# Block-causal attention into two MoE layers on one core: score units regrouped from four a pair to three, one head's evacuation fixed on VectorE, two raw weight tiles given buffers of their own

## The chip, the cores and the metric

The kernel runs on one core of a Trainium2 chip. The metric is the device time of one execution in microseconds (us); three executions of the kernel before are shown below. A core has five engines that run side by side, each in its own program order: TensorE (PE, with its weight loads shown apart as PEld), VectorE (DVE), ScalarE (ACT), GpSimd (POOL) and SyncE (SP), which here issues all the DMAs one after the other.

## The reference

Attention over 576 positions in nine blocks of 64 (a query sees its own block and those ahead of it), then two feed-forward layers with different gates. The outputs of attention are the tokens of the first layer.

```python
q, k, v: (4, 8, 576, 64)                      # batch, heads, positions, head size
scores = q @ k.T / 8
scores = where(pos_q // 64 >= pos_k // 64, scores, -1e9)
attn = exp(scores - max) / (sum + 1e-9)
x = (attn @ v) -> (2304, 512)                 # all heads side by side
h = x @ w_in;  x = (h * clip(h + 3, 0, 6) / 6) @ w_out       # first layer, d_ff 2048
h = x @ w_in2; x = (h * tanh(log1p(exp(h)))) @ w_out2        # second layer, d_ff 2048
```

## The kernel before, in words

All float32 values that go into a product are split in a high and a low part (float32r each); a product is the sum of three: high by high, high by low, low by high.

**Pairs.** The 32 heads of the four batches are taken as 16 pairs: two heads of 64 lie on 128 partitions. For each pair, `load` brings q and k, POOL scales q (L403) and splits q and k into `qs` and `ks` (L406, L290; the first pair's run partly on ACT), `scores` makes the scores of one unit in PSUM (`s`, two buffers), DVE takes the maxima (L443, `nm`), ACT the exponentials with their sums (L448, into `p`), PE transposes the result (L505, into `t`), ACT copies the high part to `z` (L284), DVE subtracts for the low part (L290), PE multiplies by the values (`attn_v`, L569, into the one buffer `o`), and ACT (L582) or DVE (L580) moves `o` to `x`. `sums` handles the sums of the exponentials (L599, L600). `x1d` and `rsd` are the DRAM homes of `x` and of the reciprocals.

**Units.** A pair has four score units. B (queries 128 to 255, keys 0 to 255), AC (queries 256 to 383 with 384 keys, and the first 128 queries with 128 keys) and D (queries 384 to 511, 512 keys) work on half rows: each head's q and k lie on 64 partitions, so a product uses 64 rows of PE's array and two heads run on the two halves. In such a unit the limit of the diagonal blocks is added at its end by a small bfloat16 product (`mask`, L478). E is the last 64 queries: those of the two heads are laid out as a block diagonal `qb` (two small DMAs a pair, 64 partitions x 2 x 64), so that its six products (L455) use all 128 rows.

**Order.** `Schedule` takes the operations in program order and decides by a planner's estimates when each engine issues what; PE's own order may shift by up to 40 operations until the first layer's first output (`plan.strict`). Units are written in the order of `UNITS`; transposes follow 2 units behind, sums 5, products with the values 6 (`LAG_T`, `LAG_R`, `LAG_V`). SP issues the DMAs in one order (L277), and one that waits for its data holds those behind it.

**Weights.** The first layer has 16 weight tiles (f = 0 to 15) that are stored packed, in two halves (c) of 512 KB, and rebuilt by ACT, POOL and DVE. For f = 0 and 1 this happens beside attention in four of the pairs (`early_weights`, `EARLY_ROUNDS`). The tiles f = 2, 3 and 4 (`first_weights`, WLOW is 2 and WMID is 4) go through one pair of raw buffers, `raw0` and `raw1`, one after another; from f = 5 on each has a raw tile that becomes free with attention's memory.

Of the kernel before, what the change touches and what calls it, by code (L numbers as in the profile page):

```python
# [41 lines left out]
E_AT = 224  # L42
ZC = 320

ORDER = tuple(range(NB))
# [5 lines left out]
EARLY_ROUNDS = (20, 28, 36, 44)  # L51
LAG_T, LAG_V, LAG_R = 2, 6, 5
# [14 lines left out]
def cost(kind, n):  # L67

    base, each = {
        "PE": (13, 0.4167), "R": (13, 0.4167), "S": (0, 0.4583), "T": (109, 0), "V": (0, 0.4583),  # L70
        "ACT": (95, 0.836), "ACT_PSUM": (50, 0.836), "EXP": (234, 0.836),
        "DVE_PSUM": (64, 1.047), "DVE": (64, 1.047), "MEMSET": (40, 0.88),
        "POOL": (145, 2.156), "POOL_ONE": (100, 0.99), "POOL_V": (260, 0.87), "SP": (100, 3.05),
    }[kind]
    return max(int(base + each * n), {"S": 105, "V": 105, "R": 215}.get(kind, 0))
# [30 lines left out]
class Schedule:  # L106

    AHEAD = 40

    def __init__(self):
        self.ops, self.writer, self.readers, self.strict = [], {}, {}, 0

# [18 lines left out]
    def order(self):  # L132
# [27 lines left out]
        done = 0  # L160
        port = {"DVE": 0, "POOL": 0}
# [10 lines left out]
        while done < n:  # L172
            best = None
            for e in names:
# [8 lines left out]
                i = min((i for i in c if ready[i] <= start), key=lambda i: (need[i], i))  # L183
                cost = took(i, e, start)
                soon = [k for k in c if start < ready[k] < start + cost and need[k] < need[i]
# [14 lines left out]
            if e == "PE":  # L200
                at += 1
                pe.remove(i)
            done += 1
# [23 lines left out]
def fused_kernel(ctx: ExitStack, tc: tile.TileContext, qT, kT, vv, w1, w2, outT):  # L227
# [75 lines left out]
    sm = pool(late, "sm", 4, side="right")  # L303
# [3 lines left out]
    for n in range(2):  # L307
# [3 lines left out]
        at["qb", n] = aq.tile([P, 2, P], F32R, tag="qb", name=f"qb{n}")  # L311
# [6 lines left out]
        for h in range(2):  # L318
            at["x", h, n] = a2.tile([P, S], F32, tag=f"x{h}", name=f"x{h}_{n}")
# [6 lines left out]
    for n in range(4):  # L326
        for c in range(2):
            at["nm", n, c] = sm.tile([P, 2], F32, tag=f"nm{c}", name=f"nm{c}_{n}")
    for u, w in (("B", 256), ("AC", 512), ("D", 512)):
        at["p", u] = ap.tile([P, 2, w], F32, tag=f"p{u}", name=f"p{u}")  # L330
# [4 lines left out]
    P_NAMES = [("p", u, i, h) for u in GROUPS for i, _, _ in GROUPS[u] for h in range(2)] + [("p", "E"), ("p", "last")]  # L335
# [4 lines left out]
        + [("qb", n, j) for n in range(2) for j in range(2)] + [("mask",), ("ones",), ("hold",)]  # L340
# [6 lines left out]
        + [("nm", n, c) for n in range(4) for c in range(2)]  # L347
# [4 lines left out]

    def load(p):
        n = p % 2
        for j in HALVES if p == 0 else (slice(0, S),):
            js = [i for i in range(2) if j.start <= HALVES[i].start < j.stop]
            for t, src in (("k", kT), ("q", qT)):
                dma((j.stop - j.start) // 2, [], [(t, n, i) for i in js], at[t, n][:, j], src[p, :, j],
                    land=LAND if p else 2600)

    def load_v(p):
        dma(320, [], [("v", p % 2)], at["v", p % 2], vv[p], land=LAND)
# [67 lines left out]
    def scores(g):  # L430
        p, u = g // NU, UNITS[g % NU]
        n, sc = p % 2, at["s", g % 2]
        qs, ks, qb, su = at["qs", n], at["ks", n], at["qb", n], at["su", n]
        half = lambda t, js: [(t, n, i, j) for i in range(2) for j in js]
        nm = [at["nm", g % 4, c] for c in range(2)]

        def maxima(c, view, to):
            width = 1
            for x in view.shape[1:]:
                width *= x  # L440
            plan.add(
                one("DVE", "DVE_PSUM", width), [("s", g % 2)], [("nm", g % 4, c)],
                lambda e: nc.vector.tensor_reduce(to, view, axis=AX.X, op=ALU.max, negate=True))  # L443

        def exps(c, h, w, a, dst, name, col):
            plan.add(
                one("ACT", "EXP", w), [("s", g % 2), ("nm", g % 4, c)], [name, ("su", n, col)],
# [3 lines left out]
        if u == "E":  # L451
            def run(e):
                for a, z in ((E_AT, 512), (512, E_AT + S)):
                    for k, (x, y) in enumerate(((0, 0), (0, 1), (1, 0))):
                        nc.tensor.matmul(  # L455
                            sc[:, a:z], qb[:, x, :], ks[:, y, a - E_AT:z - E_AT], start=k == 0, stop=k == 2)

            matmuls(6 * cost("S", S // 2), [("qb", n, j) for j in range(2)] + half("ks", (0, 1)),
                    [("s", g % 2)], run)
            maxima(0, sc[:, E_AT:E_AT + S], nm[0][:, 0:1])  # L460
            exps(0, 0, S, E_AT, at["p", u][:, 0:S], ("p", u), 8)
# [4 lines left out]
        def run(e):  # L466
            for k, (x, y) in enumerate(((0, 0), (0, 1), (1, 0))):
                for i, a, w in groups:
                    for h in range(2):
                        r = slice(64 * h, 64 * h + 64)  # L470
                        nc.tensor.matmul(
                            wide[:, h, a:a + w], qs[r, x, 128 * i:128 * i + 128], ks[r, y, 0:w],
                            start=k == 0 and a == 0, stop=False, skip_group_check=True)
            for h in range(2):
# [5 lines left out]
                    start=False, stop=True, skip_group_check=True)  # L480

        ns = sum(3 * cost("R", w) for _, _, w in groups) + 250
        js = (0,) if u == "B" else (0, 1)
        matmuls(ns, half("qs", js) + half("ks", js) + [("mask",), ("ones",)], [("s", g % 2)], run)
        for c, (i, a, w) in enumerate(groups):
            maxima(c, wide[:, :, a:a + w], nm[c])
        for c, (i, a, w) in enumerate(groups):
            for h in range(2):
                exps(c, h, w, 512 * h + a, at["p", u][:, h, a:a + w], ("p", u, i, h), 4 * h + i)
# [24 lines left out]
    def transposes(g):  # L514
        p, u = g // NU, UNITS[g % NU]
        n = p % 2
        z, x = at["z", n], at["p", u]
        chunk = lambda a: a.rearrange("p (c w) -> p c w", w=ZC)
        four = lambda tp: tp[:, 0:4, :]
        if u == "E":  # L520
# [3 lines left out]
            transpose_unit(  # L524
                n, u, 0, [x[:, c * P:c * P + P] for c in range(4)], [("p", u)], lambda tp: heads(tp, 4),
                [d[:, 0:4] for d in dst])
            plan.add(
                one("POOL", "POOL_ONE", 64), [("p", u)], [("p", "last")],
# [3 lines left out]
                n, u, 1, [x[:, 512:S + 64]], [("p", u), ("p", "last")], lambda tp: heads(tp, 1), [dst[0][:, 4:5]] * 2, slice(64, P))  # L532
        elif u == "B":
            blocks = [x[:, h, c * P:c * P + P] for h in range(2) for c in range(2)]
            transpose_unit(
                n, u, 0, blocks, [("p", u, 1, h) for h in range(2)],
                lambda tp: tp.rearrange("p (h c) q -> p h (c q)", h=2),
                [z[:, t, :, 4 * ZC:4 * ZC + 256] for t in range(2)])
        else:
            at_ = 0 if u == "AC" else P  # L540
            for h in range(2):
                transpose_unit(
                    n, u, h, [x[:, h, c * P:c * P + P] for c in range(4)],
                    [("p", u, i, h) for i, _, _ in GROUPS[u]], four,
                    [chunk(z[:, t, h])[:, 0:4, at_:at_ + P] for t in range(2)])

    def attn_v(p, r, h):
# [27 lines left out]
        a, w = ((0, 256), (256, 320))[r]  # L575
        dst, src = x[:, a:a + w], po[:, 0:w]
# [7 lines left out]
        plan.add(one("ACT", "ACT_PSUM", w) + one("DVE", "DVE_PSUM", w), [("o",)], [("x", h, n, r)], evacuate)  # L584
# [677 lines left out]
```

## Time and profile before

| what | value |
|---|---|
| median of three executions | 942.04 us (941.57 to 942.71) |
| profiled execution, its own time | 944.14 us |
| its span in the trace | 942.4 us |
| granted clock over it | 0.999 |
| PE busy | 917.9 us, 97% of the span |
| DVE busy | 606.8 us, 64% |
| POOL busy | 606.8 us, 64% |
| ACT busy | 531.9 us, 56% |

The time of an execution is a little longer than the span from the trace's first to its last instruction (944.14 against 942.4). Busy shares are means over stages with different limits: attention is the first sixth of the span, and the two layers are the rest.

### The profile page before, as it was taken

The page shows a single profiled execution, that of the slowest core. Times are in us where ns is not written, and L with a number is a line of the kernel's source. Part 1 is how long each engine was busy: PE and PEld are TensorE (multiplying, and loading weights), DVE is VectorE, ACT ScalarE, POOL GpSimd, SP SyncE. Part 2 cuts the span into 40 slices and gives each one's busy share as a digit, 9 for nine tenths or more (in the row PEclk, how much of TensorE's full clock was granted, in tenths as well). Part 3 has the DMA queues.
Part 4 walks back from the last instruction along what each step waited for, and adds up shares of the span by engine and source line. Part 5 has one row for each costly group of instructions (what it writes and reads, how often), then busy time and mean ns, then how long its engine had stood idle before and what let it go on. Part 6 is the DMA issues. An engine that isn't in the chain of part 4 may idle for free.

```text
span 942.4 us, 16053 instructions
## 1 busy us (share of the span) xinstructions
PE 917.9 (97%) x5368; PEld 830.9 (88%) x5368; DVE 606.8 (64%) x1043; ACT 531.9 (56%) x1232; POOL 606.8 (64%) x625
## 2 busy tenths in 40 slices
PE   8999999989999999999999999999999999999998
PEld 6888888868888777888888899999999999999998
DVE  6788877667954666576422244665687856866567
ACT  7899999856743546455322252644465445644452
POOL 6886775758996548645500022668798787966775
PEclk9999999999999999999999999999999999999999
DMA  6676663498287889988500038767678876696752
GB/s 209 190 224 177 165 178 87 126 312 342 102 246 263 307 272 303 314 290 281 181 1 1 0 100 295 243 247 268 228 286 315 288 268 241 250 319 241 267 207 96
DMA packets 93746, 205.61 MB, mean 218 GB/s; under 512 B 14944, under 2 KB 32992, under 8 KB 93664
## 3 DMA queue, kind: packets, MB, share of 16 engines
q1 hardware_dynamic: 93664, 204.59, 64.7%
q8 instruction: 42, 0.69, 0.3%
q14 instruction: 40, 0.33, 0.1%
HBM read 155.19 MB, written 48.31 MB: 216 GB/s over the span
## 4 chain that ended last, share of the span: by engine, by line
PE 49%; DVE 2%; POOL 2%; DMA 2%; issue 1%; ACT 1%; SPq 0%; DVEq 0%; POOLq 0%; ACTq 0%
PE y L732 8%; PE y L733 8%; PE y L734 8%; PE h L732 5%; PE h L733 5%; PE h L734 5%; PE r L732 3%; PE r L734 3%; PE r L733 3%; DMA w2d<-q 1%; POOL S L290 1%; DVE r L633 0%; DVE S L904 0%; DMA xs<-x1d 0%; POOL q L290 0%
## 5 line engine op out<-in xcount | busy, mean ns | idle before, releaser
L732 PE MATMUL h<-X,wh 128*128 128x512 f32 (+1 forms) x320 | 119.3, 373 | 2.8 <-DVE gl L290 1.2
L734 PE MATMUL h<-X,wl 128*128 128x512 f32 (+1 forms) x320 | 117.9, 368 | 1.0 <-DVE wl L785 1.0
L732 PE MATMUL y<-gh,wh 128*128 128x512 f32 (+1 forms) x320 | 117.9, 369 | 0.9 <-ACT gh L284 0.7
L733 PE MATMUL y<-gl,wh 128*128 128x512 f32 (+1 forms) x320 | 117.8, 368 | 1.0 <-POOL gl L290 1.0
L733 PE MATMUL h<-X,wh 128*128 128x512 f32 (+1 forms) x320 | 117.8, 368 | 0.0
L734 PE MATMUL y<-gh,wl 128*128 128x512 f32 (+1 forms) x320 | 117.7, 368 | 0.0
L732 PE MATMUL y<-X,wh 128*128 128x384 f32 x336 | 112.5, 335 | 1.1 <-ACT xs L284 0.9
L733 PE MATMUL y<-X,wh 128*128 128x384 f32 x336 | 112.5, 335 | 0.0
L734 PE MATMUL y<-X,wl 128*128 128x384 f32 x336 | 112.3, 334 | 0.0
L290 POOL TENSOR_TENSOR X<-xr,X 128x384 fp32r<-128x384 f32 (+2 forms) x36 | 39.3, 1095 | 104.7 <-ACT X L284 104.5
L838 DVE SCALAR_TENSOR_TENSOR h<-e,h 128x512 f32<-128x512 f32 (+1 forms) x64 | 40.1, 627 | 86.3 <-ACT e L284 86.2
L1072 DVE TENSOR_TENSOR sgh<-y,sgh 128x384 f32<-128x384 f32 x129 | 69.6, 555 | 32.9 <-PE y L734 32.8
L284 ACT ACTIVATE e<-h 128x512 f32<-128x512 f32 (+1 forms) x80 | 44.0, 550 | 69.3 <-PE h L734 69.3
L290 POOL TENSOR_TENSOR X<-e,X 128x384 fp32r<-128x384 f32 x69 | 70.9, 1028 | 10.9 <-ACT X L284 10.9
L290 DVE TENSOR_TENSOR z<-t,z 128x512 fp32r<-128x512 f32 (+1 forms) x112 | 67.8, 631 | 14.8 <-ACT z L284 13.5
L443 DVE TENSOR_REDUCE nm<-s 128x2 f32<-128x512 f32 (+4 forms) x80 | 63.1, 797 | 18.9 <-PE s L455 13.1
L732 PEld LDWEIGHTS h<-X,wh 128*128 128x128 f32 x320 | 60.3, 188 | 16.2 <-DVE gl L290 4.0
L732 PEld LDWEIGHTS y<-gh,wh 128*128 128x128 f32 x320 | 60.3, 189 | 11.7 <-ACT gh L284 1.1
L734 PEld LDWEIGHTS h<-X,wl 128*128 128x128 f32 x320 | 60.3, 188 | 11.5 <-DVE wl L785 1.4
L733 PEld LDWEIGHTS y<-gl,wh 128*128 128x128 f32 x320 | 60.3, 188 | 11.1 <-POOL gl L290 1.3
L734 PEld LDWEIGHTS y<-gh,wl 128*128 128x128 f32 x320 | 60.3, 189 | 10.0
L733 PEld LDWEIGHTS h<-X,wh 128*128 128x128 f32 x320 | 60.4, 189 | 9.5
(177 smaller groups left out, 2534.1 us busy)
## 6 DMA issues: line engine op xcount, KB each, us to landing
raw<-w SPq DMA_DIRECT2D x64, 512.0 KB
wh<-w2d SPq DMA_DIRECT2D x48, 512.0 KB
wl<-w2d SPq DMA_DIRECT2D x48, 512.0 KB
wh<-w2d SPq DMA_DIRECT2D x48, 384.0 KB
wl<-w2d SPq DMA_DIRECT2D x48, 384.0 KB
x1d<-x SPq DMA_DIRECT2D x64, 144.0 KB
w2d<-Sh SPq DMA_DIRECT2D x32, 256.0 KB
w2d<-S SPq DMA_DIRECT2D x32, 256.0 KB
```

Of the source, the lines that this page charges most:

```text
L284: nc.scalar.activation(d, s, func, **kw)
L290: engines, reads, writes, lambda e: ENG[e].tensor_sub(*real(dst, a, b)), **kw)
L443: lambda e: nc.vector.tensor_reduce(to, view, axis=AX.X, op=ALU.max, negate=True))
L732: nc.tensor.matmul(b, wh, xh, start=start and k == 0, stop=False, skip_group_check=True)
L733: nc.tensor.matmul(b, wh, xl, start=False, stop=False, skip_group_check=True)
L734: nc.tensor.matmul(b, wl, xh, start=False, stop=last, skip_group_check=True)
L838: nc.vector.scalar_tensor_tensor(g, e, 6.0, h, op0=ALU.min, op1=ALU.mult)
L1072: nc.vector.tensor_add(dst, src, old)
```

## The change

1. **Units.** `UNITS` is now AC, D, BE. The half-row unit B is gone; its two blocks of queries join the last block's in BE, all three as block diagonals on 128 rows: `qb` for blocks 2 and 3, `qe` for block 8. BE has 12 products (L477): in each of three rounds 192, 320, 256 and 256 columns. It needs no mask, since each block of queries gets just its own keys. Maxima: three of 192, 576 and 256 columns in the place of B's and E's two; exponentials: three in the place of three. The block diagonals take six small DMAs a pair in the place of two.
2. **The limit first.** In AC and D the mask product opens the group of products (L501) and the others follow (L508).
3. **Evacuation.** `o` goes to `x` on ACT for the first head and on DVE for the second, always (L617, L615).
4. **Order of tokens.** The tokens of `x` stand in another order of query blocks (`ORDER`); the host puts them back.
5. **Weights.** The raw halves of f = 2 and 3 get tiles of their own, which come free when the score stage's memory does (`leave_scores`); f = 4 alone uses `raw0` and `raw1`, and can come while attention runs. The early weights (f = 0, 1) stay with the same pairs.
6. **Planner.** It prices a switch between half-row and full-row products (`TO_ROWS`, `TO_ALL`, `KEEP`), small DMAs otherwise, shorter lags; the first load is cut at column 384, k before q, and the second pair's loads wait in the plan for the first's.

The core of the diff:

```diff
-HALVES = (slice(0, 256), slice(256, 576))
-UNITS = ("B", "AC", "D", "E")
-GROUPS = {"B": ((1, 0, 256),), "AC": ((2, 0, 384), (0, 384, 128)), "D": ((3, 0, 512),)}
+HALVES = (slice(0, 384), slice(384, 576))
+UNITS = ("AC", "D", "BE")
+GROUPS = {"AC": ((2, 0, 384), (0, 384, 128)), "D": ((3, 0, 512),)}
+BOTH = ((1, 0, 192, 0), (0, 192, 512, 192), (0, 512, 768, 192), (2, 768, 1024, 768))
-EARLY_ROUNDS = (20, 28, 36, 44)
-LAG_T, LAG_V, LAG_R = 2, 6, 5
+EARLY_ROUNDS = (15, 21, 27, 33)
+LAG_T, LAG_V, LAG_R = 2, 4, 3
@@ Schedule
+    TO_ROWS, TO_ALL, KEEP = 110, 150, 300
...
-                i = min((i for i in c if ready[i] <= start), key=lambda i: (need[i], i))
+                mode = lambda i: e == "PE" and (i in self.by_rows) != rows
+                i = min((i for i in c if ready[i] <= start), key=lambda i: (need[i] + self.KEEP * mode(i), i))
@@ load
+        after = tuple(begun) if p == 1 else ()
@@ last_queries
-            dma(32, [("qs", n, t, 1) for t in range(2)], [("qb", n, j)],
-                f32(at["qb", n][r, :, r]), f32(at["qs", n][r, :, 512:576]), land=LAND)
+            for t in range(2):
+                dma(160, [("qs", n, t, 0)], [("qb", n, j, 1 + t)], f32(at["qb", n][r, t, :, r]),
+                    f32(at["qs", n][r, t, P:2 * P]).rearrange("p (n d) -> p n d", d=64), land=LAND)
+            dma(160, [("qs", n, t, 1) for t in range(2)], [("qb", n, j, 0)],
+                f32(at["qe", n][r, :, r]), f32(at["qs", n][r, :, 512:576]), land=LAND)
@@ scores
-        if u == "E":
+        if u == "BE":
+            stationary = at["qe", n], at["qb", n][:, :, 0], at["qb", n][:, :, 1]
             def run(e):
-                for a, z in ((E_AT, 512), (512, E_AT + S)):
-                    for k, (x, y) in enumerate(((0, 0), (0, 1), (1, 0))):
+                for k, (x, y) in enumerate(products):
+                    for i, a, z, o in BOTH:
                         nc.tensor.matmul(
-                            sc[:, a:z], qb[:, x, :], ks[:, y, a - E_AT:z - E_AT], start=k == 0, stop=k == 2)
+                            sc[:, a:z], stationary[i][:, x, :], ks[:, y, a - o:z - o], start=k == 0 and a in (0, 512),
+                            stop=k == 2, skip_group_check=True)
@@ attn_v
-        plan.add(one("ACT", "ACT_PSUM", w) + one("DVE", "DVE_PSUM", w), [("o",)], [("x", h, n, r)], evacuate)
+        plan.add(
+            one("DVE", "DVE_PSUM", w) if h else one("ACT", "ACT_PSUM", w), [("o",)], [("x", h, n, r)], evacuate)
@@ raw_tile, first_weights
-                LAZY["raw", f, c] = wpool[-1].tile(
+                LAZY["raw", f, c] = wpool[1 + (f >= WMID)].tile(
-        early = f <= WMID
+        early = f == WMID
...
-    hook(leave_scores, EARLY_TILES + first)
+    hook(leave_scores, EARLY_TILES + first + [("raw", f, c) for f in range(WLOW, WMID) for c in range(2)])
```

On PE, this is a stretch of a steady pair before, from the unit D to E's products (`t` are the transposes, `o` the products with the values):

```order
L471 MATMUL s_117<-ks_115,qs_113 128x512 x6
L478 LDWEIGHTS mask
L478 MATMUL s_117<-ones,mask 128x64
L478 LDWEIGHTS mask
L478 MATMUL s_117<-ones,mask 128x64
L505 MATMUL t_144<-ident,pB 128x128 x4
L569 MATMUL o<-z_133,vh_132 128x256 x2
L569 MATMUL o<-z_133,vh_132 128x128 x2
L505 MATMUL t_142<-ident,pAC 128x128 x4
L455 MATMUL s_130<-ks_115,qb_116 128x288 x6
```

The same place after the change, from D to the first of BE's three rounds:

```order
L501 LDWEIGHTS mask
L501 MATMUL s_132<-ones,mask 128x64
L501 LDWEIGHTS mask
L501 MATMUL s_132<-ones,mask 128x64
L508 MATMUL s_132<-ks_115,qs_113 128x512 x6
L536 MATMUL t_146<-ident,pB 128x128 x4
L536 MATMUL t_144<-ident,pE 128x128 x4
L536 MATMUL t_145<-ident,pE 128x128
L477 MATMUL s_118<-ks_115,qb_116 128x192
L477 MATMUL s_118<-ks_115,qe_117 128x320
L477 MATMUL s_118<-ks_115,qe_117 128x256
L477 MATMUL s_118<-ks_115,qb_116 128x256
```

The mask stands ahead of D, the transposes of B and E of the pair before follow it together, and where E's six products stood there are twelve; the unit B, which came two groups after E, is gone.

On SP, at the program's start, these were the loads before (`q1`, `k1` are the second pair's, `v` the values):

```order
L277 DMA q0_112<-qT 128x320
L277 DMA k0_114<-kT 128x256
L277 DMA q0_112<-qT 128x256
L277 DMA k0_114<-kT 128x320
L277 DMA q1_125<-qT 128x576
L277 DMA k1_127<-kT 128x576
L277 DMA v0_118<-vv 128x640
L277 DMA qb0_116<-qs0_113 64x2x64 x2
```

And these are they after the change:

```order
L285 DMA v0_119<-vv 128x640
L285 DMA v1_133<-vv 128x640
L285 DMA raw0_160<-w1 128x1024
L285 DMA raw1_162<-w1 128x1024
L285 DMA qb0_116<-qs0_113 64x2x64
L285 DMA q1_126<-qT 128x576
L285 DMA qb0_116<-qs0_113 64x2x64
L285 DMA qe0_117<-qs0_113 64x2x64
L285 DMA qb0_116<-qs0_113 64x2x64 x2
L285 DMA qe0_117<-qs0_113 64x2x64
L285 DMA k1_128<-kT 128x576
```

Ahead of these the first pair's four loads stand as before, k now before q. The second pair's q and k, which came right behind them, now stand behind both value tiles, two raw weight tiles and the first block diagonals.

On SP, at the end of the scores, the raw tiles of f = 3 and 4 (one pair of buffers) stood before between the last outputs of attention:

```order
L277 DMA x1d_84<-x0_1_136 64x576 x2
L277 DMA raw0_157<-w1 128x1024
L277 DMA raw1_159<-w1 128x1024
L277 DMA x1d_84<-x1_1_137 64x576 x2
L277 DMA xr0_161<-x1d_84 128x512
L277 DMA xn_170<-rsd_85 64x512 x2
L277 DMA raw0_157<-w1 128x1024
L277 DMA raw1_159<-w1 128x1024
L277 DMA raw5_0_2720<-w1 128x1024
```

After the change those of f = 2 and 3 stand ahead of the last eight stores of `x`, and f = 4 came during attention:

```order
L285 DMA xn_173<-rsd_85 64x512 x2
L285 DMA raw2_0_2586<-w1 128x1024
L285 DMA raw2_1_2609<-w1 128x1024
L285 DMA raw3_0_2627<-w1 128x1024
L285 DMA raw3_1_2642<-w1 128x1024
L285 DMA rsd_85<-rs1_137 3x2x64
L285 DMA x1d_84<-x0_0_124 64x576 x2
```

Four loads of 512 KB stand together there; before, the last of them stood behind all the stores of `x`.

## Rows read from the trace of the kernel before

**Rows 1.** Stages by windows: stretch, length, PE, PEld, DVE, ACT, POOL busy, clock, DMA, GB/s.
```profile
0.00:15.09 15.09, 12.04 (x89) 10.24 (x89) 7.66 (x16) 9.43 (x26) 7.92 (x19) 1.00 0.83 260
15.09:166.61 151.52, 141.86 (x1224) 124.75 (x1223) 122.04 (x198) 140.16 (x435) 112.46 (x123) 1.00 0.59 165
166.61:206.00 39.39, 33.67 (x197) 27.20 (x197) 25.36 (x41) 26.87 (x66) 24.83 (x25) 1.00 0.67 201
206.00:300.00 94.00, 94.00 (x415) 77.83 (x416) 65.68 (x103) 56.25 (x102) 81.40 (x78) 1.00 0.71 245
```

**Rows 2.** The same view of one pair without early weights.
```profile
142.36:152.88 10.52, 10.08 (x89) 8.95 (x88) 8.24 (x14) 9.94 (x32) 7.26 (x9) 1.00 0.38 94
```

**Rows 3.** PE's timeline in that pair: start, us, instruction, idle time before it.
```profile
142.36 0.62 PE L471 MATMUL s<-ks,qs 64*128 64x256 f32 x6
142.83 0.20 PE L478 MATMUL s<-ones,mask 64*128 64x64 bf16 x2
143.36 0.66 PE L505 MATMUL t<-ident,pD 128*128 128x128 f32 x4 [0.33 <-DVE z L290]
143.77 1.37 PE L569 MATMUL o<-z,vh 128*128 128x320 f32 x9
144.97 0.66 PE L505 MATMUL t<-ident,pD 128*128 128x128 f32 x4
...
147.54 1.37 PE L569 MATMUL o<-z,vh 128*128 128x320 f32 x9
148.84 0.96 PE L471 MATMUL s<-ks,qs 64*128 64x512 f32 x6
...
151.06 1.04 PE L455 MATMUL s<-ks,qb 128*128 128x288 f32 x6
151.94 0.60 PE L505 MATMUL t<-ident,pAC 128*128 128x128 f32 x4
```

**Rows 4.** Groups by form in 15.09 to 166.61: xcount, busy us, mean ns.
```profile
L443 DVE TENSOR_REDUCE nm<-s 128x2 f32<-128x512 f32 x15 | 10.2, 681 | 0.0
L582 ACT ACTIVATE x<-o 128x320 f32<-128x320 f32 x25 | 10.9, 438 | 2.0 <-PE o L569 1.0
L443 DVE TENSOR_REDUCE nm<-s 128x2 f32<-128x256 f32 x14 | 5.9, 425 | 2.2 <-ACT pAC L448 1.2
L582 ACT ACTIVATE x<-o 128x256 f32<-128x256 f32 x25 | 9.5, 382 | 0.0
L580 DVE TENSOR_SCALAR x<-o 128x256 f32<-128x256 f32 x3 | 1.3, 418 | 0.0
L580 DVE TENSOR_SCALAR x<-o 128x320 f32<-128x320 f32 x2 | 1.0, 481 | 0.0
```

**Rows 5.** SP's DMA issues in that stretch: count, duration ns min/median/max.
```profile
L277 SPq DMA_DIRECT2D x1d<-x x52: 445/584/1082, 25.3 to 160.4; - x52
L277 SPq DMA_DIRECT2D qb<-qs x28: 599/630/671, 20.8 to 154.2; - x28
```

**Rows 6.** What SP's queue waited for there, the largest row: us, times, longest.
```profile
SPq L277 <- ACT x L582: 23.7, 22, 2.6
```

**Rows 7.** POOL's timeline at the start: the second pair's first work.
```profile
6.47 0.75 POOL L403 TENSOR_SCALAR q<-q 128x576 f32<-128x576 f32 x1 [2.12 <-DMA q<-qT]
10.10 1.41 POOL L290 TENSOR_TENSOR qs<-q,qs 128x576 fp32r<-128x576 f32 x1
```

**Rows 8.** Waits in 166.61 to 206: us in total, times, longest us.
```profile
ACT r L284 <- DMA raw<-w: 6.5, 3, 3.1
PE h L734 <- DVE wl L785: 1.0, 1, 1.0
PE y L733 <- POOL gl L290: 1.0, 1, 1.0
PE h L732 <- ACT wh L284: 0.9, 1, 0.9
```

**Rows 9.** DMA queue from 22.0 to 23.1, mostly block-diagonal pieces: packets, MB, share.
```profile
q1 hardware_dynamic: 294, 0.08, 35.5%
```

More of the change, by code (lines that the diff above doesn't have):

```diff
@@ L160, in order @@
         done = 0
+        rows = False
         port = {"DVE": 0, "POOL": 0}
@@ L202, in order @@
                 pe.remove(i)
+                rows = i in self.by_rows
             done += 1
@@ L302, in fused_kernel @@
     ap = pool(late, "ap", 1, side="right")
-    sm = pool(late, "sm", 4, side="right")
+    sm = pool(late, "sm", 3, side="right")
     ps_t = pool(late, "ps_t", 3, space=PSUM, side="right")
@@ L339, in fused_kernel @@
         + [(t, n, i, j) for t in ("qs", "ks") for n in range(2) for i in range(2) for j in range(2)]
-        + [("qb", n, j) for n in range(2) for j in range(2)] + [("mask",), ("ones",), ("hold",)]
+        + [("qb", n, j, i) for n in range(2) for j in range(2) for i in range(3)] + [("mask",), ("ones",), ("hold",)]
         + [("s", n) for n in range(2)])
@@ L466, in run @@
         def run(e):
[L467 to L473, printed above, removed]
             for h in range(2):
@@ L479, in run @@
                     out, at["mask"][r], at["ones"][r, 0:64 * len(groups)].rearrange("p (g n) -> p g n", n=64),
[L480 to L484, printed above, removed]
+                    start=True, stop=False, skip_group_check=True)
+            for k, (x, y) in enumerate(products):
+                for i, a, w in groups:
+                    for h in range(2):
+                        r = slice(64 * h, 64 * h + 64)
+                        nc.tensor.matmul(
+                            wide[:, h, a:a + w], qs[r, x, 128 * i:128 * i + 128], ks[r, y, 0:w],
+                            start=False, stop=k == 2, skip_group_check=True)
+        ns = sum(3 * cost("R", w) for _, _, w in groups) + (90 if u == "AC" else 60)
+        js = (0,) if u == "AC" else (0, 1)
+        plan.by_rows.add(
+            matmuls(ns, half("qs", js) + half("ks", js) + [("mask",), ("ones",)], [("s", g % 2)], run))
         for c, (i, a, w) in enumerate(groups):
@@ L523, in transposes @@
                 z[:, t].rearrange("p h (c w) -> p c h w", w=ZC)[:, :, :, 256:ZC] for t in range(2)]
-            transpose_unit(
-                n, u, 0, [x[:, c * P:c * P + P] for c in range(4)], [("p", u)], lambda tp: heads(tp, 4),
-                [d[:, 0:4] for d in dst])
             plan.add(
-                one("POOL", "POOL_ONE", 64), [("p", u)], [("p", "last")],
+                one("POOL", "POOL_ONE", 64), [("p", "E")], [("p", "last")],
                 lambda e: nc.gpsimd.tensor_scalar(
@@ L677, in fused_kernel @@
         if 0 <= u < NP:
-            attn_v(u, i // 2, i % 2)
-            if i == 3 and u + 2 < NP:
+            for m in V_AT[i]:
+                attn_v(u, m // 2, m % 2)
+            if i == NU - 1 and u + 2 < NP:
                 split_v(u + 2)
```

128 lines of the change are left out of this document (78 added, 50 removed).

## The prediction

> **What bounds the kernel now.** I read the stages first [rows 1]. From 206 us on, PE is busy for 94.00 of 94.00 us, and the change touches nothing that is issued later, so I leave that part as it is. Everything is decided in the first 206 us, and they have three parts.
>
> Up to 15.09 us, where the second pair's AC begins, PE has work for 12.04 us. From 15.09 to 166.61 (the AC of the last pair) lie 14 pairs, 151.52 us, or 10.82 a pair: PE is busy 141.86, ACT 140.16, DVE 122.04, POOL 112.46. From 166.61 to 206 attention ends and the first layer begins; there PE has 33.67 us of work in 39.39, so it stands for 5.72.
>
> A pair without early weights takes 10.52 us [rows 2]: PE 10.08, ACT 9.94, DVE 8.24, POOL 7.26. Two engines are nearly full. PE's timeline of that pair [rows 3] shows one wait with a name, 0.33 us for DVE's low part of `z`; the other 0.11 of the 0.44 us that PE idles are too small to be named. So PE sets the pace, with ACT just behind it, and neither can gain much unless both are relieved. The four pairs with early weights make up the rest: 151.52 less 14 times 10.52 is 4.24, about 1.06 us each.
>
> **The change, part by part.** *PE.* From the timeline [rows 3], the unit B takes from 142.36 to the next transposes at 143.36, less the wait of 0.33: 0.67 us with its mask. E takes from 151.06 to 151.94, 0.88 us for 6 x 288 = 1,728 columns. Together 1.55. BE streams 3 x (192 + 320 + 256 + 256) = 3,072 columns; at E's price for a column that is 0.88 x 3,072 / 1,728 = 1.56. So joining the units gives PE nothing by itself. What it saves is one passage from full rows to half rows: from the nine products with the values to D it takes 148.84 - 147.54 = 1.30 us, to transposes 144.97 - 143.77 = 1.20, so 0.10 each. The way back and the mask's new place have no row of their own; I bound them by nothing and by the whole 0.20 that two mask products show in B, and take 0.05 for both. PE's work per pair falls by 0.1 to 0.15, to about 9.95.
>
> One rule speaks against this part. The row says that B costs 0.67. The Trainium skill (TensorEngine Tiling (Array Packing), Theoretical Speedup) says that a contraction of 64 or less, run as two row tiles, goes up to twice as fast; by it block diagonals on full rows waste half of the array. It would price B's products at 768 columns, 0.39 us, and BE's additional 1,344 columns at 0.68, a loss of 0.29 a pair, or +4 us over 14 pairs. By the row the sum is even, since the fixed parts of the unit eat what the halves give; I go by the row.
>
> *ACT.* Evacuations took 25 x 438 + 25 x 382 ns in 14 pairs [rows 4], 1.46 us a pair; afterwards one of each size is left, 0.82. With 64 columns less in the exponentials ACT comes to 9.94 - 0.64 - 0.05, about 9.25 in a clean pair.
>
> *DVE.* It gets 0.418 + 0.481 = 0.90 us of evacuation a pair and had (3 x 0.418 + 2 x 0.481) / 14 = 0.16, so +0.74. Of the maxima, B's over 512 columns (681 ns) goes; one of 256 (425 ns) and one of 192 come, the latter by the slope between those two rows 0.36: +0.10. So 8.24 + 0.84 = 9.1.
>
> All three main engines then lie between 9.1 and 9.95. If PE kept no wait at all, a clean pair would take 9.95; I put 0.1 of its old 0.44 back, since DVE, on which it waited, gets fuller, and take 10.05. The pairs with early weights take 1.06 more now; ACT, which does a part of them, is freed by 0.69, DVE is fuller, and I take 10.7 where it was 11.58. Ten pairs at -0.47 and four at -0.88 are -8.2; not every pair will reach that, so **-7.5**. The bounds are -3 (PE's waits all stay and DVE adds some) and -11 (9.95 in clean pairs and 10.2 with early weights).
>
> *SP and the DMAs.* Four more block-diagonal DMAs a pair, each like those now of 630 ns [rows 5], are +2.5 us of issue in a pair. The queue has slack: for ACT's `x` alone it stood 23.7 us in the 14 pairs [rows 6], 1.7 a pair, and for others besides. Nothing waits for a block diagonal as long as it comes within the pair ahead. In bytes it is small: 294 packets, nearly all pieces of a block diagonal, took 35.5% of 16 engines for 1.1 us [rows 9], 21 ns each; 512 more are 10.9 us spread over 16 engines, 0.7 us a pair, beside a DMA share of 0.38 [rows 2]. I cost it at nothing; what hides it is that slack, and the price without it is a rival below.
>
> *Start.* POOL begins the second pair at 6.47 us, on the arrival of its q, and ends the last split of it at 10.10 + 1.41 = 11.51 [rows 7], 5.04 later. Afterwards 590 KB of the first pair, 655 KB of values, 1,049 KB of weights and a first block diagonal of 33 KB stand ahead of that q (295 KB): 2.62 MB. At the stage's 260 GB/s [rows 1] the bytes that had moved by 6.47 are 1.68 MB, so q would come 0.94 / 0.26 = 3.6 us later if transfers run side by side, at 10.1, and the splits end at 15.1: just when AC begins today. If they come strictly one after another (now 0.885 MB had to come by 6.47, so the first byte moved at 3.1), q comes at 13.2, the splits end at 18.2, and AC is 3.1 us late. Between 0 and +3.1 I take **+1.5**. k stands still further back.
>
> *End of the scores.* ACT waits 6.5 us for raw weights, and PE three times about 1 us for `wl`, `gl` and `wh` [rows 8]; these, and the waits for gates that hang behind them, are most of the 5.72. With tiles f = 2 and 3 in their own buffers the raw data comes as soon as the scores end, some 8 us sooner than today's f = 3. I let 3.65 of the 5.72 go. The last pair has its B behind 166.61 now and had it ahead: BE in E's place adds 0.68. **-3.0**, with -4.5 and +0.7 (nothing recovered) as bounds.
>
> The sum: +1.5 - 7.5 - 3.0 = -9.0. The profiled execution had 944.14, so about 935.1; the median shown is 942.04, 2.1 lower, so **933.0**.
>
> **Rivals.** *DVE takes the pace.* With 9.1 us of work, some of it in an order that PE waits for (the low parts of `z` are its only named wait now), waits come back: 10.4 in a clean pair and 10.9 with early weights give -1.2 - 2.7 = -3.9, and with start and end -5.4: 936.6. For it: 0.33 stands there today [rows 3]. Against: ACT, from which DVE waits too, is freed.
>
> *Slower: SP's queue.* The additional 2.5 us of issue exceed the 1.7 that the wait for `x` shows. If the rest of the slack is no help, because it lies at the wrong places, each pair grows by 0.8: k, q and block diagonals come late and BE waits. That is +11 at full size; at half size +5.6, with +1.5 and -3.0 it gives +4.1: 946. It decides from about 0.1 us a pair above today's 10.82 on. Against: the loads are a pair ahead, and the period is still longer than SP's added work needs.
>
> *No gain in attention.* B's products alone took 142.83 - 142.36 = 0.47 us [rows 3]; if its mask and its passages were hidden and cost nothing, BE's additional 1,344 columns at 0.68 make each pair 0.21 dearer, the waits that fall away pay for it, and the pace goes to 10.45: -1.0 in clean pairs, -1.0 with early weights, +1.5 at the start and -0.5 at the end, because the raw weights were hidden anyway: 941. The tiling rule of the Trainium skill points this way.
>
> *Only the rest fails.* The start costs its 3.1 and the end gives +0.7 while attention gains 7.5: -3.7, 938.3.
>
> **How the numbers follow.** The forecast has 0.60, DVE's pace 0.13, SP's queue 0.11, no gain 0.08, the failing ends 0.08. Its own range is 928.5 to 937; with DVE, the ends and part of the case without gain the range for 8 in 10 is 928.5 to 940.5. A measurement of this kernel tells some 0.2% (1.9 us) from no change. Faster: 0.60 + 0.13 + 0.08 = 0.81. Same: 0.08. Slower: 0.11.
>
> **What the profile after would show.** Right: AC to AC near 10.05 us in clean pairs, B's removal paid by BE of 1.5 us, ACT near 9.25 and DVE near 9.1 in them, no PE wait above 0.2 us in a clean pair, less than 2.5 us of idle PE where attention hands over, and work from there on as long as before. Wrong: PE waits for the block diagonals or for k in BE (SP's queue), waits for `z` from DVE above 0.4 a pair, an AC of the second pair later than 18 us, or PE waits for f = 2, whose raw data now comes only when the scores end.

## The result and the profile after

The changed kernel takes 933.75 us in the median of four executions (932.92 to 934.64), the kernel before 942.38 beside it: a ratio of 0.9903, with an interval of 0.988 to 0.9927. It is faster by 8.6 us; 9.0 had been forecast. The profiled execution had 933.24 us with a span of 931.4, against 942.4 before. This is the page's line of busy time:

```profile
PE 915.3 (98%) x5336; PEld 835.5 (90%) x5336; DVE 611.7 (66%) x1080; ACT 521.3 (56%) x1207; POOL 612.4 (66%) x634
```

The stages by windows, with the same marks as [rows 1]: the second pair's AC begins at 17.80 us, the third's at 28.78, the last's at 159.05, and 195.00 lies as far from the span's end as 206.00 did before. In the 94 us from there on PE is busy throughout, as it was.

```profile
0.00:17.80 17.80, 12.98 (x75) 11.22 (x77) 6.89 (x15) 7.56 (x20) 9.69 (x23) 0.90 0.73 225
17.80:28.78 10.98, 8.81 (x61) 7.13 (x61) 7.25 (x14) 7.56 (x26) 9.76 (x12) 0.84 0.44 114
28.78:159.05 130.27, 128.40 (x1120) 118.02 (x1120) 119.12 (x217) 122.97 (x388) 106.83 (x116) 1.00 0.70 195
159.05:195.00 35.95, 33.77 (x216) 28.98 (x216) 27.67 (x48) 28.02 (x71) 23.33 (x24) 1.00 0.77 240
```

The start is 17.80 - 15.09 = 2.71 us longer. The 14 pairs take 10.98 + 130.27 = 141.25 us in the place of 151.52, 10.27 less. The handover takes 35.95 in the place of 39.39, 3.44 less. +2.71 - 10.27 - 3.44 is -11.0, which is the difference of the two spans.

The mark needs one caution. AC now begins with its mask product, and the second pair's other products may still wait for `ks`. By the third pair's AC the start is 28.78 - 25.70 = 3.08 us longer, and the 13 pairs from there to the last took 140.91 us before and take 130.27 now, 10.64 less. This is the line of before:

```profile
25.70:166.61 140.91, 132.47 (x1145) 116.85 (x1144) 112.66 (x183) 130.95 (x406) 102.86 (x112) 1.00 0.59 167
```

Windows of one pair without early weights and of one with them:

```profile
38.57:48.33 9.76, 9.76 (x87) 9.09 (x86) 8.81 (x16) 9.07 (x30) 7.38 (x10) 1.00 0.57 133
58.10:68.69 10.59, 10.12 (x88) 9.04 (x88) 9.93 (x18) 9.60 (x31) 8.54 (x10) 1.00 0.64 169
```

PE is now busy for all of a clean pair: 9.76 of 9.76, where it had 10.08 of 10.52 [rows 2]. In the pair with early weights DVE is the fullest beside PE, 9.93 of 10.59. From PE's timeline of a clean pair (139.51 to 149.28):

```profile
142.70 0.27 PE L636 MATMUL t<-ident,su 128*9 128x128 f32 x1
142.73 1.38 PE L600 MATMUL o<-z,vh 128*128 128x320 f32 x9
144.04 0.20 PE L501 MATMUL s<-ones,mask 64*128 64x64 bf16 x2
144.08 0.94 PE L508 MATMUL s<-ks,qs 64*128 64x512 f32 x6
144.95 0.66 PE L536 MATMUL t<-ident,pB 128*128 128x128 f32 x4
145.44 0.71 PE L536 MATMUL t<-ident,pE 128*128 128x128 f32 x5
145.91 0.34 PE L477 MATMUL s<-ks,qb 128*128 128x192 f32 x1
...
147.47 0.57 PE L600 MATMUL o<-z,vh 128*128 128x256 f32 x4
```

BE reaches from 145.91 to 147.47: 1.56 us. No row of PE has a wait in the pair. E's five transposes take 145.91 - 145.44 = 0.47, and the transpose of the sums 0.03 ahead of the next product. Before, the same work took from 146.64 to the next products at 147.54 [rows 3], 0.90 us. These are its rows on PE and, last, the weight load of the transpose of the sums on PEld:

```profile
146.64 0.76 PE L505 MATMUL t<-ident,pE 128*128 128x128 f32 x5
147.51 0.28 PE L600 MATMUL t<-ident,su 128*9 128x128 f32 x1
147.51 0.09 PEld L600 LDWEIGHTS t<-ident,su 128*9 128x9 f32 x1 [0.35 <-DVE su L599]
```

The same work takes 0.50 now, so 0.40 us of a wait stood there. No row of PE names it, but PEld's does: 0.35 us for the reciprocals of the sums (`su`), which DVE makes. Of the 0.40, 0.11 lay in the 0.44 us that PE was seen to idle, and 0.29 inside its busy time, since the ends of its products are modelled. With the 0.33 for `z` [rows 3] this is 0.73 of the 0.75 us that a clean pair became shorter; both waits were for DVE, and both are gone. PE's waits from the third pair's AC to the last's, before and after:

```profile
PE s L455 <- ACT pAC L448: 3.6, 5, 0.8
PE t L505 <- DVE z L290: 3.0, 10, 0.3
PE t L505 <- DVE val L633: 0.8, 2, 0.4
```

```profile
PE s L477 <- ACT pAC L467: 1.9, 4, 0.5
```

One kind is left, one of 0.5 us in each pair with early weights. It stands ahead of BE, for the exponentials of AC:

```profile
65.29 0.36 PE L477 MATMUL s<-ks,qb 128*128 128x192 f32 x1 [0.47 <-ACT pAC L467]
```

E's transposes began at 64.09 there, so they and the wait took 1.20 us where a clean pair has 0.47: 0.73 of the 0.82 us that such a pair is longer.

### The profile page after: what moved, and what is told of

Same layout as the page of the kernel before. It is cut to its first block, busy times and chain, and to the rows that moved or that the text cites. A ratio compares the mean times of both kernels' runs of the same rounds, so it can differ in the third digit from the quotient of the medians.

```text
span 931.4 us, 16127 instructions
## 1 busy us (share of the span) xinstructions
PE 915.3 (98%) x5336; PEld 835.5 (90%) x5336; DVE 611.7 (66%) x1080; ACT 521.3 (56%) x1207; POOL 612.4 (66%) x634
## 4 chain that ended last, share of the span: by engine, by line
PE 77%; POOL 6%; DMA 5%; DVE 5%; ACT 3%; issue 2%; SPq 1%; POOLq 0%; DVEq 0%; ACTq 0%
PE y L772 11%; PE y L773 11%; PE y L774 11%; PE h L772 8%; PE h L773 8%; PE h L774 8%; PE o L600 4%; PE t L536 4%; PE s L477 3%; PE r L773 3%; PE r L772 3%; PE r L774 3%; PE s L508 2%; DMA w2d<-q 1%; POOL S L298 1%
## 5 line engine op out<-in xcount | busy, mean ns | idle before, releaser
L298 POOL TENSOR_TENSOR X<-e,X 128x384 fp32r<-128x384 f32 x69 | 70.8, 1027 | 10.9 <-ACT X L292 10.9
L298 DVE TENSOR_TENSOR z<-t,z 128x512 fp32r<-128x512 f32 (+1 forms) x112 | 67.2, 629 | 11.7 <-ACT z L292 10.7
L774 PEld LDWEIGHTS h<-X,wl 128*128 128x128 f32 x320 | 60.4, 189 | 10.3 <-DVE wl L825 0.2
L462 DVE TENSOR_REDUCE nm<-s 128x2 f32<-128x768 f32 (+2 forms) x96 | 62.1, 676 | 8.5 <-PE s L508 3.8
```

Source lines behind the costliest of these rows:

```text
L298: engines, reads, writes, lambda e: ENG[e].tensor_sub(*real(dst, a, b)), **kw)
L774: nc.tensor.matmul(b, wl, xh, start=False, stop=last, skip_group_check=True)
```

## The experiments

An execution of one and the same program differs by a few microseconds from the next (the changed kernel had 932.4 to 936.8 in one series), so the stages of the profiled executions carry most of what follows, and the medians are given beside them. The kernel before had medians of 943.08 to 943.89 us beside them, so across experiments the ratios are compared.

**The evacuation alone, and the units without it.** Before, with the second head fixed on VectorE:

```diff
-        plan.add(one("ACT", "ACT_PSUM", w) + one("DVE", "DVE_PSUM", w), [("o",)], [("x", h, n, r)], evacuate)
+        plan.add(
+            one("DVE", "DVE_PSUM", w) if h else one("ACT", "ACT_PSUM", w), [("o",)], [("x", h, n, r)], evacuate)
```

> The kernel before with the second head's evacuation fixed on VectorE, and nothing else. Theory: relief of ACT alone does not make the four units faster, since PE waits for DVE's low parts and DVE gets 0.74 us a pair more: the 14 pairs stay within 1.5 us of 151.5, the whole within 2 us of before. Rival: ACT set the pace, and its 0.64 us less in a pair gives 3 us or more.

Measured: 943.51 us, ratio 0.9999 (0.9983 to 1.0014). From the second pair's AC to the last's:

```profile
15.71:170.45 154.74, 142.17 (x1211) 123.48 (x1211) 128.63 (x220) 134.60 (x420) 139.41 (x145) 1.00 0.65 197
```

```profile
PE t L505 <- DVE z L290: 3.5, 9, 1.3
PE s L471 <- ACT pB L448: 3.2, 4, 0.8
PE s L455 <- ACT pAC L448: 2.2, 5, 0.5
PE o L569 <- ACT x L582: 2.0, 8, 0.3
```

ACT's work fell from 140.16 to 134.60, DVE's rose from 122.04 to 128.63, and the 14 pairs took 3.2 us longer than 151.52; the "within 1.5" was too narrow, and the rival (3 us gained) is out. PE's waits in 26.31 to 170.45 are of four kinds and 10.9 us, where before they were of three and 7.4; the one for `x` is new, since `o` has only one buffer.

The edit is one line, but the planner made another order from it. POOL's work in the 14 pairs rose from 112.46 to 139.41 us, because operations of the first layer (`xr`, `X`, `wl`) were drawn ahead. The handover became shorter, 32.45 us instead of 39.39:

```profile
170.45:202.90 32.45, 31.24 (x199) 26.99 (x199) 24.26 (x41) 21.48 (x55) 9.01 (x11) 1.00 0.51 147
```

So the 154.74 is not the pace alone. A clean pair without that work, from 159.68 to 170.45, took 10.77 us where it was 10.52, with PE waiting 0.24 for `x` and 0.28 for `z`. Relief of ACT alone left the whole as it was, and the clean pairs at the end of attention slower.

The other half is the changed kernel with the same two lines undone.

> The changed kernel, but the planner chooses the engine of each evacuation again, as in the kernel before. Theory: the regrouped units took PE's waits away and ACT's relief is only a help: a clean pair stays within 0.1 us of 9.77 and the whole within 1.5 us of 933.75. Rival: ACT sets the pace as soon as it has the evacuations back: 0.4 to 0.6 us more on ACT in each pair, a clean pair at 10.1 or more, 4 to 6 us in all.

Measured: 941.06 us, ratio 0.9984 (0.9965 to 1.0002).

```profile
15.90:169.79 153.89, 141.71 (x1180) 125.95 (x1180) 124.81 (x222) 137.27 (x423) 124.71 (x133) 0.99 0.69 189
```

```profile
PE s L477 <- ACT pAC L467: 4.5, 9, 0.5
PE t L536 <- DVE z L298: 2.5, 4, 0.6
PE o L600 <- DVE z L298: 2.4, 4, 0.7
```

My theory fell: the 14 pairs took 153.89 us, not 141, and the rival, ACT's pace, came nearer, though it had 4 to 6 us in all and 7 were lost. In a clean pair (148.74 to 159.25, 10.51 us) PE issues the same groups in the same order as in the changed kernel, each as long as there but for one place, ahead of BE:

```profile
154.67 0.71 PE L536 MATMUL t<-ident,pE 128*128 128x128 f32 x5
155.87 0.36 PE L477 MATMUL s<-ks,qb 128*128 128x192 f32 x1 [0.49 <-ACT pAC L467]
```

1.20 us stand there instead of 0.47: 0.73 of the 0.74 that the pair is longer. PE's two old waits for DVE are gone in this pair too. BE's scores need the buffer `s` that AC's exponentials empty. ACT did those exponentials in one stretch in the changed kernel, from 143.59 to 145.48; here an evacuation and a copy to `z` stand between them, and they last from 152.82 to 155.82:

```profile
153.38 0.43 ACT L617 ACTIVATE x<-o 128x320 f32<-128x320 f32 x1
154.87 0.60 ACT L292 ACTIVATE z<-t 128x512 fp32r<-128x512 f32 x1 [0.15 <-PE t L536]
155.62 0.20 ACT L467 ACTIVATION_READ_ACCUMULATOR pAC<-s,nm 128x1 f32 x1
```

ACT was busy for 9.59 us here and for 9.07 to 9.58 in the clean pairs of the changed kernel, so here it is the order in its queue that costs, not its work. So of the 10.3 us in attention the regrouping without the fixed evacuation brings none, nor does the fixed evacuation on the kernel before; together they bring all.

**Three parts of the change on the old units.** Evacuation, the limit first and the raw tiles, on the kernel before.

```diff
+                    start=True, stop=False, skip_group_check=True)
+            for k, (x, y) in enumerate(((0, 0), (0, 1), (1, 0))):
...
-        early = f <= WMID
+        early = f == WMID
```

> The kernel before with three parts of the change (evacuation of the second head on VectorE, the limit's product first, raw weights of f = 2 and 3 in their own tiles), but with its four units and its planner. Theory: the units carry the pace: clean pairs stay at 10.3 or above, the 14 pairs gain less than 4 us of the 10.3 that the whole change gained, the handover gains 2 to 3.5 us, and the whole is near 936 to 939. Rival: the relief of ACT carries the pace: clean pairs at 10.0 or below, and 932 to 935 in all.

Measured: 938.84 us, ratio 0.9955 (0.9939 to 0.9971).

```profile
14.83:168.16 153.33, 140.85 (x1211) 120.45 (x1210) 128.91 (x220) 135.03 (x420) 138.38 (x143) 1.00 0.66 201
168.16:200.70 32.54, 31.11 (x198) 26.43 (x198) 25.04 (x43) 22.90 (x58) 12.07 (x15) 1.00 0.61 181
```

The whole lies where the theory put it, but not as it said: the 14 pairs gained nothing (153.33), and all of the 4.3 us (943.14 beside it) come from the rest. In the handover (200.70 lies as far from the span's end as 206.00 did) PE stands for 32.54 - 31.11 = 1.43 us, where it stood for 5.72. That is not the raw tiles' doing alone: work of the first layer was drawn ahead as in the run before_evac (POOL 138.38), where PE stood for 1.21 without them. The run keeps the old planner and its lags with the old units, so it does not tell which of these the pace needs; the new planner with the old units was not tried.

**The raw weights.** Alone on the kernel before:

```diff
-                LAZY["raw", f, c] = wpool[-1].tile(
+                LAZY["raw", f, c] = wpool[1 + (f >= WMID)].tile(
...
-        early = f <= WMID
+        early = f == WMID
```

> The kernel before with one part of the change alone: raw halves of f = 2 and 3 in tiles of their own, f = 4 loaded beside attention. Theory: this part alone is worth 3 to 7 us where attention hands over (39.39 us before) and leaves the 14 pairs at 151.5 us within 1.5: the whole near 936 to 939. Rival: it is worth less than 1.5 us, and the handover gains with the units alone: above 940.5.

Measured: 937.76 us, ratio 0.9939 (0.9925 to 0.9954).

```profile
15.00:166.50 151.50, 141.80 (x1224) 124.65 (x1223) 122.01 (x198) 140.14 (x435) 112.48 (x123) 1.00 0.58 165
166.50:199.50 33.00, 30.14 (x184) 24.93 (x184) 20.99 (x36) 25.94 (x65) 24.46 (x25) 1.00 0.76 230
```

Attention is as it was to 0.02 us; the handover, by the same mark at its end, falls from 39.39 to 33.00 us, and its idle PE from 5.72 to 2.86. Here POOL's work in attention stayed as it was. What ACT and POOL waited for raw weights in the handover fell from 15.0 us (6.5, 4.9 and 3.6) to 0.7. The theory holds: this part alone gives some 5 us. The same part undone in the changed kernel:

> The changed kernel with the raw halves of f = 2, 3 and 4 in one pair of buffers again. Theory: raw weights that come late are what PE waited for where attention hands over to the first layer: that stage grows by 2.5 to 3.5 us (from 35.95) and so does the whole, to 936.5. Rival: the gain of 3.4 us there comes from the shorter attention and the new order of the last units: then it grows by less than 1 us.

Measured: 932.19 us, ratio 0.9894 (0.9871 to 0.9917). By the median nothing was lost, so the theory fell for the whole. The profiled execution, the longest of four (935.07), did have a long handover, with another wait in it:

```profile
155.84:197.00 41.16, 37.42 (x221) 31.79 (x220) 26.34 (x45) 26.09 (x67) 22.55 (x24) 0.92 0.67 199
```

```profile
PE t L536 <- POOL pE L557: 3.7, 1, 3.7
```

PE waited 3.7 us for a small copy by POOL. POOL's queue had stood 6.8 us for a load of stored outputs (`xr`, DMA `xs`) ahead of that copy, and the granted clock of the stage fell to 0.92. The changed kernel itself had the same in another execution (the run after_again, below: POOL 5.7 us for `xs`, PE 1.1 for that copy), so it need not come from the shared buffers. Together with the other order of loads at the start (below):

> The changed kernel with the order of loads of start_order and one pair of raw buffers for f = 2, 3 and 4 as in raw_shared. Theory: with the units and the evacuations of the change, the raw tiles of their own are worth nothing, since their four loads fall together where attention's last stores are made, and the start gains 1 to 2 us: near 930 to 931.5, the lowest of all. Rival: the raw tiles are worth 3 to 5 us here too (handover of 39 us and more), and the whole lies above 934.

Measured: 935.65 us, ratio 0.9915 (0.9899 to 0.9932). PE's waits in the handover:

```profile
PE y L776 <- POOL gl L300: 2.5, 1, 2.5
PE t L539 <- POOL pE L560: 2.0, 1, 2.0
```

The time is the rival's (above 934), and so is the handover of 41.9 us, with waits for POOL in it; but the changed kernel had 934.16 beside it. By the ratios it is some 2 us more than each of its two edits alone (0.9915 against 0.9891 and 0.9894), but the intervals overlap. What the raw tiles are worth inside the changed kernel therefore stays open between a loss of 0.8 us (0.9894 against 0.9903) and a gain of 2.3 (0.9915 against 0.9891); neither is clear of noise.

**The start.** The loads of the second pair put ahead of the values, block diagonals ahead of the raw weights:

```diff
-        after = tuple(begun) if p == 1 else ()
...
-                        land=LAND if p else 2600, after=after)
+                        land=LAND if p else 2600, behind=begun[-1:] if p < 2 else ())
...
-            w1[f, :, 512 * c:512 * c + 512].bitcast(U32), land=LAND)
+            w1[f, :, 512 * c:512 * c + 512].bitcast(U32), land=LAND, behind=begun[-1:])
```

> The changed kernel with another order of its first loads: k and q of the first pair, k and q of the second, the first values, the first pair's block diagonals, and only then the second values and the two raw weight tiles. Theory: the order of the loads costs the start. Then the second pair's AC begins near 15 us and not at 17.80, the granted clock of the first 20 us stays at 1.00, and the whole is 2 to 3.5 us shorter than the changed kernel (near 931 us). Rival: the block diagonals come late because they hang behind the split of q, whatever stands in the queue, and BE is late by that alone: then AC stays above 17 us and the whole within 1 us of 933.75.

Measured: 932.31 us, ratio 0.9891 (0.9869 to 0.9914). POOL began the second pair at 7.14 us and not at 13.60, and its AC came at 12.83; but the third's came at 28.50, hardly sooner than 28.78. Here is what was gained and lost, by windows of start_order:

```profile
2.00:10.00 8.00, 6.22 (x46) 5.19 (x45) 4.00 (x7) 2.44 (x8) 4.76 (x11) 1.00 0.75 220
10.00:18.00 8.00, 7.38 (x41) 6.35 (x41) 3.18 (x6) 4.53 (x15) 5.18 (x7) 0.59 0.76 233
18.00:26.00 8.00, 4.98 (x28) 3.66 (x27) 4.78 (x9) 5.64 (x19) 6.99 (x8) 0.77 0.63 198
```

The mean granted clock was 0.59 and 0.77: for part of these windows PE ran at the lower of its two levels (1.2 and 2.4 GHz), after it had stood from 8.5 to 9.9 us. So the transfers come in time, and the time is lost all the same: part of it at the lower clock (BE of the first pair took 2.88 us, and 1.82 at a clock of 1.00 in after_again), and 2.70 us in a wait of PE for BE's exponentials on ACT. Filling the gap with idle work was the test of that:

```diff
+            if g == 1:
+                matmuls(1300, [("s", 1)], [("t", 0)], lambda e: fill())
...
+    def fill():
+        for n in range(12):
+            nc.tensor.transpose(at["t", 0][:, n % 4, :], ident, ident)
```

> The changed kernel with 12 transposes of the identity, whose results nothing reads, put on PE behind the first pair's D, where PE stands for 1.3 us until the first exponentials are done. Theory: the start loses time since the clock falls when PE idles from 8.5 to 12 us; with that gap filled the granted clock stays at 1.00 up to 26 us, the third pair's AC comes at 25 to 26.5 us and not at 28.78, and the whole is 1 to 3 us shorter in the median. Rival: the late block diagonals and k alone make the start long: then AC stays above 27.5 us and the whole within 1 us of 933.75.

Measured: 940.8 us, ratio 0.9973 (0.9955 to 0.999). The clock fell all the same (0.58 from 14 to 18 us), AC of the third pair came at 28.01, and the planner, which counts the fill as work, ordered a later pair worse: from the sixth to the seventh AC it was 13.42 us and not 10.59. The edit doesn't test the clock by itself, since it also moves the plan.

> The same filling together with the order of loads of the run start_order (28.50 us to the third pair's AC, at half clock from 12 to 18 us). Theory: order and clock together make the start: AC of the third pair at 24 to 26 us, the whole near 929 to 931 us. Rival: what comes sooner on one side is lost on the other (BE behind AC of the second pair, exponentials in one queue): above 27 us, and no better than 932.

Measured: 938.5 us, ratio 0.9945 (0.9929 to 0.9961). The clock stayed at 1.00 up to 18 us and fell to 0.54 behind that; AC of the third pair came at 27.83. That is the rival's side, and no way to gain the start.

**The kernel itself again.**

> The changed kernel itself once more, to see what of its trace repeats. Theory: the pace repeats to 0.05 us (clean pairs 9.77, those with early weights 10.59), while the start does not: the second pair's AC came at 17.80 us in one trace and at 15.14 in the run raw_shared, whose start has the same instructions; the whole lies between 932 and 935. Rival: the start's 17.80 us repeats too, to 0.5 us.

Measured: 934.16 us, ratio 0.9901 (0.9884 to 0.9918), six executions from 932.4 to 936.77. Its windows, to be read beside those of after:

```profile
0.00:15.60 15.60, 12.00 (x74) 9.93 (x76) 6.78 (x15) 7.57 (x20) 8.49 (x22) 1.00 0.78 239
15.60:25.83 10.23, 7.44 (x61) 5.97 (x62) 7.06 (x14) 7.82 (x26) 10.06 (x13) 1.00 0.58 147
25.83:156.09 130.26, 128.38 (x1119) 118.01 (x1120) 119.10 (x217) 122.98 (x388) 105.49 (x115) 1.00 0.70 192
156.09:196.80 40.71, 37.81 (x226) 32.32 (x226) 29.74 (x52) 29.12 (x72) 27.63 (x29) 0.96 0.79 252
```

The theory holds: 13 pairs take 130.26 us here and 130.27 there. The start does not repeat: with the clock at 1.00 the third pair's AC comes at 25.83, as before (25.70); with 0.90 and 0.84 it came at 28.78. Part of that is not the clock: PE waited 1.51 us for the first block diagonal there and 0.27 here. Nor does the handover repeat: 40.71 us against 35.95, with the clock at 0.96. Start and handover of one and the same program thus differ by 3 and 5 us, so a profile of a single execution cannot price a part of the change in them to better than that.

**The limit's product last**, in AC and D of the changed kernel: its loop stands behind that of the other products again, with these flags:

```diff
-                    start=True, stop=False, skip_group_check=True)
+                    start=False, stop=True, skip_group_check=True)
```

> The changed kernel with the limit's product at the end of AC and D again. Theory: it is worth 0.03 to 0.05 us a unit, as AC and D took 1.03 and 0.91 us against 1.08 and 0.94, so clean pairs come to 9.85 and the whole is 1.1 us longer, near 935. Rival: it is worth nothing, within 0.3 us (pace 9.77).

Measured: 934.19 us, ratio 0.9904 (0.9888 to 0.9921). From the fourth pair's mask product to the last's, 12 pairs by the same rows, 38.95 to 160.37 is 121.42 us; in after it is 38.57 to 159.05, 120.48. That is 0.08 us a pair, as expected, 1.1 us over 14, too little for the whole to show.

**SP's queue.** Four more DMAs like the block diagonals' in every pair, into a tile that nobody reads:

```diff
+            for t in range(2):
+                dma(160, [("qs", n, t, 0)], [("junk", j, t)], at["junk"][r, t, :].rearrange("p (n d) -> p n d", d=64),
+                    f32(at["qs", n][r, t, P:2 * P]).rearrange("p (n d) -> p n d", d=64), land=LAND)
```

> The changed kernel with four more DMAs of the block diagonals' shape in every pair, into a tile that nothing reads. SP issues for 8.3 us and waits for 1.5 us in a pair of 9.77 now; four more are 2.5 us. Theory: the queue has no more room than that, and a pair cannot be shorter than its issues: 10.8 us or more, 12 to 18 us in all. Rival: SP's waits and issues overlap with enough slack that the pace stays within 0.2 us of 9.77, and the whole within 3 us.

Measured: 970.61 us, one execution. The AC of the third to sixth pairs still follow each other by 9.77 us (26.99, 36.77, 46.53, 56.30); from there on a pair takes 10.8 to 14.5. What waited for what from 60 to 166 us:

```profile
POOL vh L450 <- DMA v<-vv: 16.7, 8, 3.4
ACT x L621 <- DMA x1d<-x: 12.8, 7, 3.5
POOL ks L429 <- DMA k<-kT: 11.6, 7, 3.4
...
PE o L604 <- ACT x L621: 5.7, 6, 1.4
```

The loads are ahead for some pairs and hide it so long; then values, keys and stores are late, and `o` is not emptied, since `x` is not yet stored. The pace is as the theory said, 10.8 and more, but the whole lost 37 us and not 12 to 18. From the sixth pair's AC to the last's it took 180.04 - 56.30 = 123.74 us where the changed kernel took 100.95, 2.3 us more in each of ten pairs. Another 16.4 us were lost behind the last pair's AC, in a handover of 52.36 us at a clock of 0.90. The rival of the prediction is real; the changed kernel stands just short of it.

## Why the prediction was right

**The sum** was right to 0.4 us in the difference of the medians, and that is in part luck. The stages of the two profiles add up to -11.0 where the forecast had -9.0. Every stage lies within its bounds in that profile, but the terms were off on both sides, and in the second profile of the same program (after_again) the handover, +1.3, lies outside them.

*Attention* was forecast at -7.5, and -10.3 came (clean pairs 9.77 and not 10.05, early ones 10.59 and not 10.7), within the bound of -11. The step that failed is "PE's work per pair falls by 0.1 to 0.15, to about 9.95". It took 10.08 as PE's work, and 0.29 of that was the hidden part of the wait for the reciprocals. The work itself hardly fell: 0.75 us were gained, and 0.73 of them are the two waits for DVE. The limit first gave 0.08 a pair, and PE's other groups together became 0.06 longer, so the saved passage from full rows to half rows shows in no sum. I also put 0.1 of the old wait back on account of DVE; nothing came back. What I costed by rows was right: BE 1.56 for 1.55 of B and E, so the regrouping by itself gave PE's products nothing; ACT 9.07 to 9.58 for 9.25, DVE 8.81 for 9.1. By the Trainium skill (TensorEngine Tiling (Array Packing), Theoretical Speedup) a contraction of 64 gains up to twofold from two row tiles, and the estimate worked out from it was a loss of 0.29 us a pair; BE's 1.56 us beside the 1.55 do not show it.

One reading was wrong: "The four pairs with early weights make up the rest". Before, from the third pair's AC on, nine clean pairs took 10.52 to 11.17 us and the four with early weights 10.94, 10.94, 11.56 and 11.56, not 11.58 each. So the nine clean pairs gained 8.0 us and the four others 2.6, where the forecast had 4.7 for ten and 3.5 for four.

The mechanism was "neither can gain much unless both are relieved", and the runs bear out that two things are needed, but not that a full ACT was the reason. With the new units and their plan PE's waits for DVE go (evac_either, clean pair); with the evacuation fixed as well, ACT's exponentials no longer hold BE up. The fixed evacuation is shown by an edit of its own, 12.6 us in attention and 7 in the whole (ratio 0.9984 without it, 0.9903 with it). The other half is not: the units came together with the planner's prices and the shorter lags, and which of them let the transpose of the sums stand without a wait was not tested.

*The start* was +1.5 between 0 and +3.1. By the third pair's AC it was +3.1 in one trace and +0.1 in another of the same program. The step "q comes later" is right (POOL began at 13.60 us and 12.68 instead of 6.47), but loads in another order did not cure it. I had not counted with the clock: with a mean granted clock of 1.00 from 8 to 26 us the third pair's AC came at 25.4 and 25.8 us (raw_shared, after_again), with 0.91 at 26.4 and 26.6 (start_raw, evac_either), with 0.81 or less at 27.8 to 28.8 in five traces and at 26.99 in one (qb_plus4). Which comes first there, the waits or the clock, no run separates.

*The handover* was -3.0, and -3.4 came in the profile (idle PE 5.72 to 2.18) and +1.3 in the second one. The mechanism was right on the kernel before, where the raw tiles alone took 2.86 us of idle PE away and gave some 5 us. In the changed kernel their part is open.

*The rivals.* DVE did not take the pace in clean pairs. In pairs with early weights it is full (9.93 of 10.59), but the wait that PE has there is for ACT's exponentials, 0.73 of the 0.82 us more. SP's queue did not slow the kernel: it waited 23.7 us for `x` before [rows 6] and 1.8 after, while its issues grew, and 2.5 us more a pair would have been too much.

## What to carry to other kernels

- Where engines wait for each other in turn, a part that relieves one of them may measure as nothing, and another part as nothing, and the two together as the whole gain; test them together before either is dropped.
- PE's busy time can hold waits that no row of PE names. Take a group's price from start to start against the same group elsewhere, and read the waits of the weight loads (PEld) beside PE's.
- Where a planner orders everything, an edit of one line moves work between stages; look at what each engine does in the stage before its length is called a pace.
- A queue that issues ahead hides an overload for as many pairs as it is ahead; look at the late pairs, not at the first.

## What the runs showed of the hardware

- The same instructions at the start ran with a granted clock of 1.00 in one execution and at 0.90 and 0.84 (mean of the first two stages) in another, 3 us apart by the third pair. The fall came after PE had stood several times between 8 and 14 us, 3.5 us in all; in the other execution it had stood there 2.2 us.
- Four DMAs of 64 partitions x 2 x 64 more in each pair (some 0.6 us of issue each) made the last ten pairs 2.3 us longer each, nearly all of their issue time, while the DMA engines' mean busy share was 0.60 (56.30 to 180.04). The pairs from the third to the sixth showed nothing of it.
